# mLSTM and mixture of experts on one core: order of the gate activations, place of one gate broadcast, PSUM banks of the state update, and order of the w2 rounding

## The chip, the cores and the metric

One NeuronCore of one Trainium2 chip runs the program. The metric is the time of one execution on the device in microseconds (us). TensorE is called PE in the profile, VectorE DVE, ScalarE ACT, GpSimd POOL, and SyncE, which issues the DMA transfers, SP.

## The reference, cut to what matters

Sixteen heads (2 batches of 8) run a gated recurrence over 768 steps with 40 columns each; its output, normalised and gated by a sigmoid, is the input x (1536 rows of 320) of four dense experts, whose outputs are weighted and added.

```python
for t in range(S):                                   # S = 768, D = 40, 16 heads
    m_new = np.maximum(f_gate[:, :, t] + m, i_gate[:, :, t])
    f_stab = np.exp(f_gate[:, :, t] + m - m_new)
    i_stab = np.exp(i_gate[:, :, t] - m_new)
    m = m_new
    C = f_stab * C + i_stab * einsum('bhd,bhe->bhde', vt, kt)
    n = f_stab * n + i_stab * kt
    y[:, :, t] = sigmoid(o_gate) * (C @ q) / max(|n.q|, 1)
for e in range(E):                                   # 4 experts, F = 1024
    out += p[:, e:e+1] * (np.maximum(x @ w1[e], 0) @ w2[e])
```

## The kernel before

**Chunks.** The recurrence is cut into 12 chunks of 128 steps, numbered n = 0 to 11, with batch b = n % 2 and place in time c = n // 2. For a chunk, `spread(n)` (PE, for n = 0 to 3) or `load_f(n)` (a DMA that broadcasts from the DRAM copy `f_d`, for n >= 4) puts the forget gates of eight heads on all partitions (tile fb). `decay(n)` on DVE runs two scans over fb (four heads each, line 441) that give the decay matrix dd. `scores(n)` on PE multiplies k by q, `weigh(n)` on DVE multiplies by dd (tile pm), `intra(n)` on PE multiplies pm by the scaled values. `values(n)` and `keys(n)` on POOL scale v (tile vp) and k (tile kp). `state(n)` on PE adds the chunk to the state: its PSUM tile st is added on DVE (line 500, two instructions) to `cd`, the decayed old state from `carry` on POOL, and the sum is cs. `inter(n+1)` on PE reads the state of the other batch, and ACT scales it (yb, eight instructions). `norm(n)` on DVE makes the gated row block, `turn(n)` transposes it on PE (tile px), ACT rounds it to fp32r (xst, xd), and `turn_lo(n)` on DVE stores the remainder.

**Experts between the chunks.** While the recurrence runs, the first expert is computed for the finished rows: `PLAN[n]` lists what step n of the loop issues after its own chunk work. "H03" is `hidden` (products with w1, then `relu`) of row block 0, feature pair 3; "O00" is the output product with w2 for pair 0; "D" is one half of `decay(n + 2)`; "T" is `turn(n)`. All weights are held as a rounded value and a remainder: `split_w2` lets ACT write the rounded part (line 104) and POOL the remainder (line 107). After the loop the other row blocks and experts 1 to 3 follow.

**Order.** Each engine runs its instructions in the order in which the code issues them; nothing is reordered. Semaphores make one engine wait for another. PSUM tiles come in pairs from pools: tag "y" (`ps_y`) holds st, y1 of `inter` and y0 of `intra`, tag "w" (`ps_w`) holds the two tiles of `scores` and px of the loop's `turn`. A tile gets the slot whose last user came earliest, and waits for that user's readers.

**Activations.** ACT needs a table load (line 413 or 625 of the timeline) between Exp and Sigmoid; Copy and Relu run with either. Gates of the first chunks use Exp (lines 312, 322), then `gate_o(0)` a sigmoid of chunks 0 and 1, then Exp for the other chunks (line 625 and 322), and later sigmoids (`gate_o(1)` and on). `gate_o` works in place in acc: acc holds output gates until the rows' results replace them, and its rows 8 to 11 are filled by `load_o(4)` and `load_o(5)` late in the loop.

Of the kernel before, what the change touches and what calls it, by code (L numbers as in the profile page):

```python
# [18 lines left out]
L = 128  # L19
NC = S // L  # L20
# [15 lines left out]
NPE = 4  # L36

PLAN = {
    2: "H03 O00 T",
    3: "D O01 D O02 T",  # L40
    4: "D H10 D H11 O03 T",
    5: "D H12 D H13 O10 T",
# [14 lines left out]
def tile_mlstm_moe(ctx, tc, gt, qk, vk, ot, dp, w1, w2, out):  # L57
# [185 lines left out]
    with ExitStack() as actx:  # L243
# [56 lines left out]
        def gate_max(c0, c1):  # L300
            g = slice(c0 * L, c1 * L)
            nc.vector.tensor_tensor_scan(
                out=mb[:, c0 * L + 1:c1 * L + 1], data0=gat[:, 0, g], data1=gat[:, 1, g],
                initial=-1e30 if c0 == 0 else mb[:, c0 * L:c0 * L + 1],
                op0=ALU.add, op1=ALU.max,
            )
# [111 lines left out]
        def spread(n, pool, tag):  # L418

            b, c = n % B, n // B  # L420
            fbs[n] = [pool.tile([L, 4, L], F32, tag=tag, name="fb") for _ in range(2)]
            for h in range(H):
                nc.tensor.matmul(  # L423
                    fbs[n][h // 4][:, h % 4, :],
                    sel[:, b * H + h:b * H + h + 1].to_broadcast([L, L]),
                    fr[:, c * L:(c + 1) * L], start=True, stop=True,
                )

        def load_f(n):
            b, c = n % B, n // B  # L430
            fb = a0.tile([L, H, L], F32, tag=f"fb{n % 2}", name="fb")
            fbs[n] = fb[:, 0:4], fb[:, 4:8]
            nc.sync.dma_start(
                fb, f_d[b * H:(b + 1) * H, c * L:(c + 1) * L].unsqueeze(0).to_broadcast([L, H, L])
            )
# [41 lines left out]
            for r in range(2):  # L477
                nc.vector.tensor_mul(pm[:, r], ss[n][r], dd[:, r])  # L478

        def state(n, pool=ps_y, tag="y"):  # L480

            b, c, vv, kk = n % B, n // B, vvs[n], kp[n % 2]
            if c == NC - 1:
                return
            st = pool.tile([L, NP, L], F32, tag=tag, name="st")
            blocks = [(slice(64 * r, 64 * r + D), slice(64 * r, 64 * r + D + 1)) for r in range(2)]
            for p in range(NP):
                for r, (q, q2) in enumerate(blocks):
                    h = 2 * p + r
                    nc.tensor.matmul(  # L490
                        st[q, p, q2], kk[:, h], vv[:, h, 0:D + 1], start=True, stop=True
                    )
            cout = cs[b]
            if c == 0:
                for q, q2 in blocks:
                    copy(nc.scalar, cout[q, :, q2], st[q, :, q2])
            else:
                cd = cds.pop(n)
                for q, q2 in blocks:
                    nc.vector.tensor_add(cout[q, :, q2], cd[q, :, q2], st[q, :, q2])  # L500
# [107 lines left out]
        gate_pair(0, 1, nc.vector)  # L608
        nc.scalar.activation(even, par.unsqueeze(2).to_broadcast([L, 2, 64]), AF.Copy)
        gate_max(1, NC)  # L610
        spread(0, ps_h, "ph")
        spread(1, ps_o, "po")
        keep_warm(256, ps_w, "w")
        scores(0)
        gate_t(0, 1)
        pits.pop(0)
        g1, m1, mp1 = slice(L, S), mb[:, L + 1:S + 1], mb[:, L:S]
        nc.gpsimd.tensor_add(fs[:, g1], gat[:, 0, g1], mp1)
        values(0)
        values(1, HI)  # L620
        gate_o(0)
        decay(0)
        decay(1)
        nc.gpsimd.tensor_sub(fs[:, g1], fs[:, g1], m1)
        nc.scalar.activation(fs[:, g1], fs[:, g1], AF.Exp)
        for _ in range(2):
            keep_warm(256, ps_y, "y")
        scores(1, ps_h, "ph")
        weigh(0)
        weigh(1)  # L630
        gate_i(1, NC, nc.gpsimd)
        values(1, LO)
        intra(0)
        gate_starts(1, NC, nc.gpsimd)
        gate_pair(1, 2, nc.gpsimd)
        nc.sync.dma_start(f_d, fs)
        w2r = raws.tile([L, NF, DM], F32, tag="raw", name="w2r")
        nc.sync.dma_start(w2r, w2[0])
        load_vk(1)
        load_o(1)  # L640
        quarter_hi(0)
        quarter_lo(0)
        quarter_hi(1)
# [39 lines left out]
        keys(2)  # L683
        carry(2)
        first.corners(4)
        first.relu(4)
        inter(2, ps_o, "po")
        gate_o(1)
        split_w2(w2s, 0, 2, w2r, nc.gpsimd)
        gctx.close()  # L690
        a0 = actx.enter_context(
            tc.tile_pool(name="a0", bufs=1, side="right", reuse_waits="tile")
        )
        load_f(NPE)
        load_f(NPE + 1)

        def step(a):
            w, k = work[int(a[1])], int(a[2])
# [6 lines left out]
        for n in range(2, NCH):  # L705
            j, cc = n // 2, n % 2
            plan = PLAN[n].split()
            nxt = n + 1 < NCH
            if cc == 0 and j + 1 < NG:
                load_qk(j + 1)  # L710
                load_vk(j + 1)
            if NPE + 2 < n + 3 < NCH:
                load_f(n + 3)
            if cc == 0:
                if j > 1:
                    gate_o(j)
                if j + 1 < NG:
                    load_o(j + 1)
            if n == NCH - 2:
                raw1 = load_w1e(1)  # L720
            state(n)
            if n > 2:
                turn_lo(n - 1)
            if nxt:
                inter(n + 1)
            intra(n)
            norm(n)
            if n == 3:
                decay(NPE)
                load_f(NPE + 2)  # L730
            if nxt:
                scores(n + 1)
            for a in plan:
                if a[0] == "H":
                    work[int(a[1])].corners(int(a[2]) // 2 * 4)
                    break
            if nxt:
                values(n + 1)
                keys(n + 1)
                weigh(n + 1)  # L740
                carry(n + 1)
            if n < 4:
                for f in ((2, 4), (6,))[n - 2]:
                    split_w2(w2s, f, 2, w2r, nc.gpsimd)
            if n == 2:
                psum_e = const.tile([L, NCH, 1], F32, name="psum_e")
                nc.gpsimd.tensor_add(psum_e, pw[:, :, 0:1], pw[:, :, 1:2])
                for e in range(2, NE):
                    nc.gpsimd.tensor_add(psum_e, psum_e, pw[:, :, e:e + 1])
                nc.gpsimd.tensor_scalar_add(psum_e, psum_e, 1e-9)  # L750
            if n == 3:
                nc.vector.reciprocal(psum_e, psum_e)
                nc.gpsimd.tensor_mul(pw, pw, psum_e.to_broadcast([L, NCH, NE]))
            half = 0
            for a in plan:
                if a == "T":
                    turn(n, ps_w, "w")
                elif a == "D":
                    decay(n + 2, half)
                    half = 1  # L760
                else:
                    step(a)
# [103 lines left out]
```

## Time and profile before

| what | value |
|---|---|
| median of three runs | 413.05 us (412.98, 413.05, 414.2) |
| the profiled execution: its own time | 414.11 us |
| its span, first to last instruction | 412.3 us |
| PE busy | 400.2 us (97%) |
| DVE, ACT, POOL busy | 175.5, 130.0, 80.3 us |
| slices of the span (40 of 10.3 us) with a granted clock under nine tenths | one, the sixth (51.5 to 61.8 us): six tenths |

The span is shorter than the execution by 1.81 us. A busy share is a mean over stages: up to about 127 us the recurrence and the first expert share the engines, behind it only the experts are left.

### The profile page before, as it was taken

The page shows a single profiled execution, that of the slowest core. Times are in us where ns is not written, and L with a number is a line of the kernel's source. Part 1 is how long each engine was busy: PE and PEld are TensorE (multiplying, and loading weights), DVE is VectorE, ACT ScalarE, POOL GpSimd, SP SyncE. Part 2 cuts the span into 40 slices and gives each one's busy share as a digit, 9 for nine tenths or more (in the row PEclk, how much of TensorE's full clock was granted, in tenths as well). Part 3 has the DMA queues.
Part 4 walks back from the last instruction along what each step waited for, and adds up shares of the span by engine and source line. Part 5 has one row for each costly group of instructions (what it writes and reads, how often), then busy time and mean ns, then how long its engine had stood idle before and what let it go on. Part 6 is the DMA issues. An engine that isn't in the chain of part 4 may idle for free.

```text
span 412.3 us, 7152 instructions
## 1 busy us (share of the span) xinstructions
PE 400.2 (97%) x3042; PEld 361.9 (88%) x3042; DVE 175.5 (43%) x313; ACT 130.0 (32%) x312; POOL 80.3 (19%) x93
## 2 busy tenths in 40 slices
PE   9898599999999999999999999999999999999996
PEld 6698599989998898998988988989989889889896
DVE  7885977778842403313214134133142251231321
ACT  3958314444433533205213033034031140120210
POOL 2976722130000720002410010006100010000000
PEclk9999969999999999999999999999999999999999
DMA  6967457285000112100300003002100000001001
GB/s 175 338 225 202 123 159 198 85 232 203 3 2 2 58 70 102 52 2 0 129 0 2 0 2 153 2 0 74 55 0 2 0 2 32 33 0 50 16 16 49
DMA packets 15000, 29.34 MB, mean 71 GB/s; under 512 B 1000, under 2 KB 10760, under 8 KB 13656
## 3 DMA queue, kind: packets, MB, share of 16 engines
q1 hardware_dynamic: 14968, 28.88, 21.9%
q8 instruction: 24, 0.39, 0.4%
q14 instruction: 8, 0.07, 0.1%
HBM read 26.86 MB, written 2.02 MB: 70 GB/s over the span
## 4 chain that ended last, share of the span: by engine, by line
PE 87%; DVE 5%; issue 3%; POOL 2%; ACT 2%; DVEq 0%; POOLq 0%; ACTq 0%
PE ph L164 39%; PE po L224 39%; PE y L534 3%; PE s L472 2%; DVE dd L441 2%; PE pwm L84 1%; DVE cs L500 1%; PE fb L423 1%; POOL w1s L107 1%; PE px L561 1%; DVE pm L478 1%; POOL kp L461 1%; POOL cd L506 0%; PE st L490 0%; POOL w2s L107 0%
## 5 line engine op out<-in xcount | busy, mean ns | idle before, releaser
L164 PE MATMUL ph<-xst,w1s 128*128 128x512 f32 (+3 forms) x840 | 175.4, 365 | 0.2 <-DVE xst L569 0.2
L224 PE MATMUL po<-w2s,h 128*128 128x320 f32 x1152 | 173.3, 310 | 0.7 <-POOL w2s L107 0.7
L224 PEld LDWEIGHTS po<-w2s,h 128*128 128x128 f32 x1152 | 169.8, 188 | 2.4 <-POOL w2s L107 0.9
L164 PEld LDWEIGHTS ph<-xst,w1s 128*128 128x128 f32 (+1 forms) x840 | 142.1, 190 | 28.3 <-issue 4.4
L207 ACT ACTIVATE h<-ph 128x512 fp32r<-128x512 f32 x96 | 57.4, 599 | 206.1 <-PE ph L164 206.1
L208 DVE SCALAR_TENSOR_TENSOR h<-ph,h 128x512 fp32r<-128x512 f32 x96 | 66.1, 690 | 105.7 <-ACT h L207 105.2
L234 DVE SCALAR_TENSOR_TENSOR acc<-po,pw,acc 128x320 f32<-128x320 f32 x36 | 19.8, 551 | 99.9 <-PE po L224 99.9
L107 POOL TENSOR_TENSOR w1s<-raw,w1s 128x512 fp32r<-128x512 f32 (+1 forms) x24 | 23.6, 1023 | 96.9 <-ACT w1s L104 96.9
L441 DVE TENSOR_TENSOR_SCAN dd<-fb,id 128x512 f32<-128x512 f32 x24 | 30.4, 1293 | 0.1
L107 POOL TENSOR_TENSOR w2s<-raw,w2s 128x640 fp32r<-128x640 f32 x6 | 9.5, 1577 | 98.2 <-ACT w2s L104 98.2
L534 PE MATMUL y<-vp,pm 128*64 128x41 f32 x384 | 14.5, 237 | 6.5 <-DVE cs L500 5.5
L534 PEld LDWEIGHTS y<-vp,pm 128*64 128x64 f32 x384 | 13.3, 145 | 8.4 <-issue 4.0
L526 ACT ACTIVATE yb<-y,ibT 128x41 f32<-128x41 f32 x80 | 15.9, 311 | 1.5 <-ACT xd L565 1.0
L164 PE MATMUL ph<-xd,w1s 64*128 64x512 f32 (+1 forms) x56 | 16.2, 397 | 0.0
L478 DVE TENSOR_TENSOR pm<-s,dd 128x512 f32<-128x512 f32 x24 | 15.3, 682 | 0.1
L472 PE MATMUL s<-qk 64*128 64x128 f32 (+1 forms) x192 | 15.0, 296 | 0.0
L104 ACT ACTIVATE w2s<-raw 128x640 fp32r<-128x640 f32 x12 | 8.8, 733 | 16.5 <-DMA raw<-in_w 16.5
L455 POOL TENSOR_TENSOR vp<-vk,ibT 128x320 f32<-128x320 f32 x12 | 9.6, 799 | 22.3 <-PE y L534 12.8
L472 PEld LDWEIGHTS s<-qk 64*128 64x128 f32 (+1 forms) x192 | 12.8, 199 | 1.1 <-issue 0.7
L461 POOL TENSOR_TENSOR kp<-vk,dd 128x320 f32<-128x320 f32 x10 | 7.4, 740 | 23.8 <-DVE dd L441 23.8
L232 ACT ACTIVATE acc<-po,pw 128x320 f32<-128x320 f32 x12 | 6.3, 528 | 15.5 <-PE po L224 15.5
L104 ACT ACTIVATE w1s<-raw 128x512 fp32r<-128x512 f32 (+1 forms) x24 | 11.2, 517 | 0.0
(87 smaller groups left out, 187.1 us busy)
## 6 DMA issues: line engine op xcount, KB each, us to landing
raw<-in_w SPq DMA_DIRECT2D x3, 1536.0 KB, 8.8
fb<-f_d SPq DMA_DIRECT2D x8, 512.0 KB, 4.7
raw<-in_w SPq DMA_DIRECT2D x3, 1280.0 KB, 5.5
qk<-in_qk SPq DMA_DIRECT2D x4, 832.0 KB
vk<-in_vk SPq DMA_DIRECT2D x5, 640.0 KB, 10.1
acc<-in_ot SPq DMA_DIRECT2D x6, 320.0 KB, 9.9
out<-acc SPq DMA_DIRECT2D x12, 160.0 KB, 1.8
qk<-in_qk SPq DMA_DIRECT2D x4, 416.0 KB
```

Source lines behind the costliest of these rows:

```text
L104: nc.scalar.activation(hi, raw, AF.Copy)
L107: eng.tensor_sub(lo, raw, hi.bitcast(F32))
L164: nc.tensor.matmul(self.banks[i][:, f % self.nf, :], self.w1s[r, wi, f * L:(f + 1) * L], x[r, self.t0:self.t0 + self.n], start=(i not in s ...
L207: nc.scalar.activation(hh, ph, AF.Relu)
L208: nc.vector.scalar_tensor_tensor(out=hl, in0=ph, scalar=0.0, in1=hh.bitcast(F32), op0=ALU.max, op1=ALU.subtract)
L224: nc.tensor.matmul(po, self.hs[f][a][:, sl], ws[:, b, f, :], start=(first and i == 0), stop=(last and i == len(ks) - 1),)
L234: nc.vector.scalar_tensor_tensor(out=acc[:, i, :], in0=po, scalar=pw[:, i, e:e + 1], in1=acc[:, i, :], op0=ALU.mult, op1=ALU.add,)
L441: nc.vector.tensor_tensor_scan(out=dds[n][:, 4 * i:4 * i + 4].rearrange("p h t -> p (h t)"), data0=fbs[n][i].rearrange("p h t -> p (h t)") ...
L472: nc.tensor.matmul(ss[n][r][:, p, :], kg[q, p], qg[q, p], start=True, stop=True)
L478: nc.vector.tensor_mul(pm[:, r], ss[n][r], dd[:, r])
L526: nc.scalar.activation(yb[:, h], y1[:, h, 0:D + 1], AF.Copy, scale=ibT[:, c, i:i + 1])
L534: nc.tensor.matmul(y[t, h, 0:D + 1], pms[n][:, h, t], vvs[n][:, h, 0:D + 1], start=True, stop=True,)
```

## The change

It has five parts. (1) The exponentials of all chunks are issued before the first sigmoid, on POOL and ACT; `gate_t(0, 1)` moves between the two spreads; the v scaling of chunk 0 on POOL comes behind the gates' subtractions, and that of chunk 1 behind the gate pair; one more dummy product (`keep_warm`) stands before `scores(1)`. (2) The forget gates of chunk 4 are loaded early, into acc rows 8 to 11, so that `decay(4)` can run in step 2 of the plan; `decay(5)` alone stays in step 3. (3) `state(n)` takes a slot of tag "w", not "y". (4) `first.relu(4)` moves from ahead of the loop to behind `state(2)`. (5) The w2 roundings move: pair 0 ahead of the loop, pair 2 ahead of chunk 3's values in step 2, pair 4 ahead of chunk 4's in step 3, pair 6 behind them; the sum over the experts' probabilities moves one step back.

```diff
-    2: "H03 O00 T",
+    2: "D H03 D O00 T",
...
+        load_f(NPE, acc[:, 8:12].rearrange("p c d -> p (c d)")[:, 0:H * L]
+               .rearrange("p (h t) -> p h t", h=H))
...
-        def state(n, pool=ps_y, tag="y"):
+        def state(n, pool=ps_w, tag="w"):
...
         spread(0, ps_h, "ph")
+        gate_t(0, 1)
+        pits.pop(0)
         spread(1, ps_o, "po")
+        values(0, HI)
+        values(1, HI)
+        gate_f(1, NC, nc.gpsimd)
+        gate_i(1, NC, nc.gpsimd)
+        values(0, LO)
+        decay(0)
+        decay(1)
         keep_warm(256, ps_w, "w")
         scores(0)
...
-        for _ in range(2):
+        for _ in range(3):
             keep_warm(256, ps_y, "y")
         scores(1, ps_h, "ph")
+        gate_o(0)
...
-        first.relu(4)
         inter(2, ps_o, "po")
         gate_o(1)
...
             state(n)
-            if n > 2:
+            if n == 2:
+                first.relu(4)
+            else:
                 turn_lo(n - 1)
...
-            if n == 3:
-                decay(NPE)
-                load_f(NPE + 2)
...
+            if n == 2:
+                split_w2(w2s, 2, 2, w2r, nc.gpsimd)
+            if n == 3:
+                split_w2(w2s, 4, 2, w2r, nc.gpsimd)
             if nxt:
                 values(n + 1)
                 keys(n + 1)
```

On DVE, in step 2 and the start of step 3, the program before stands like this (from the weighting of chunk 3 to its norm; h is the remainder of a relu, line 569 and 570 are `turn_lo(2)`):

```order
L478 TENSOR_TENSOR pm<-s,dd 128x4x128 x2
L208 SCALAR_TENSOR_TENSOR h<-ph,h 128x512
L500 TENSOR_TENSOR cs_133<-cd,st 40x4x41 x2
L569 TENSOR_TENSOR xst<-px,xst 128x2x128
L570 TENSOR_TENSOR xst<-px,xst 64x128
L547 TENSOR_TENSOR y_678<-y_678,yb 128x8x41
```

and in the changed kernel:

```order
L479 TENSOR_TENSOR pm<-s,dd 128x4x128 x2
L442 SCALAR_TENSOR_TENSOR dd<-acc,id_121 128x512
L208 SCALAR_TENSOR_TENSOR h<-ph,h 128x512
L442 SCALAR_TENSOR_TENSOR dd<-acc,id_121 128x512
L501 TENSOR_TENSOR cs_133<-cd,st 40x4x41 x2
L570 TENSOR_TENSOR xst<-px,xst 128x2x128
L571 TENSOR_TENSOR xst<-px,xst 64x128
L548 TENSOR_TENSOR y_677<-y_677,yb 128x8x41
```

The two scans of `decay(4)`, which read the gates from acc, moved ahead of the state update of chunk 3 and of `turn_lo(2)`. They were behind the norm of chunk 3, ahead of the weighting of chunk 4.

On POOL, from the work of chunk 2 to the sum over the experts, the program before has these rows (vp, kp and cd of chunks 2, 3 and 4; w2s is a remainder of w2):

```order
L455 TENSOR_TENSOR vp_128<-vk,ibT 128x8x40
L461 TENSOR_TENSOR kp_130<-vk,dd 128x320
L506 TENSOR_TENSOR cd<-cs_132,bl 104x512
L107 TENSOR_TENSOR w2s_97<-w2r,w2s_97 128x640
L455 TENSOR_TENSOR vp_129<-vk,ibT 128x8x40
L461 TENSOR_TENSOR kp_131<-vk,dd 128x320
L506 TENSOR_TENSOR cd<-cs_133,bl 104x512
L107 TENSOR_TENSOR w2s_97<-w2r,w2s_97 128x640 x2
L747 TENSOR_TENSOR psum_e<-pw 128x12
```

and the changed kernel these:

```order
L456 TENSOR_TENSOR vp_128<-vk,ibT 128x8x40
L462 TENSOR_TENSOR kp_130<-vk,dd 128x320
L507 TENSOR_TENSOR cd<-cs_132,bl 104x512
L107 TENSOR_TENSOR w2s_97<-w2r,w2s_97 128x640 x2
L456 TENSOR_TENSOR vp_129<-vk,ibT 128x8x40
L462 TENSOR_TENSOR kp_131<-vk,dd 128x320
L507 TENSOR_TENSOR cd<-cs_133,bl 104x512
L107 TENSOR_TENSOR w2s_97<-w2r,w2s_97 128x640
L456 TENSOR_TENSOR vp_128<-vk,ibT 128x8x40
L462 TENSOR_TENSOR kp_130<-vk,dd 128x320
L507 TENSOR_TENSOR cd<-cs_132,bl 104x512
L107 TENSOR_TENSOR w2s_97<-w2r,w2s_97 128x640
```

Two w2 remainders now stand ahead of chunk 3's vp and kp, where there was one, and one each ahead of chunk 4's and behind it.

On ACT, the same stretch read before (yb of chunks 2 and 3, the sigmoid into acc, the w2 roundings):

```order
L207 ACTIVATE h<-ph 128x512
L526 ACTIVATE yb<-y_495,ibT 128x41 x8
L413 ACT_TABLE_LOAD
L413 ACTIVATE acc<-acc 128x640
L104 ACTIVATE w2s_97<-w2r 128x640
L526 ACTIVATE yb<-y_539,ibT 128x41 x8
L453 ACTIVATE vp_129<-ibT 128x8
L104 ACTIVATE w2s_97<-w2r 128x640 x2
```

and now, behind a first rounding of w2 that stands ahead of these rows:

```order
L527 ACTIVATE yb<-y_496,ibT 128x41 x8
L413 ACTIVATE acc<-acc 128x640
L207 ACTIVATE h<-ph 128x512
L527 ACTIVATE yb<-y_542,ibT 128x41 x8
L104 ACTIVATE w2s_97<-w2r 128x640
L454 ACTIVATE vp_129<-ibT 128x8
```

The table load is gone here, the relu came behind the first yb, and the rounding that the second POOL remainder needs stands behind the second yb.

## Rows read from the trace of the kernel before

**Rows 1.** Chain that ended last, its last stage: start, us, what.

```profile
127.77 14.05 PE ph L164 x62
...
409.17 0.55 DVE acc L234
```

**Rows 2.** Who waited for whom, PE: us in total, times, longest.

```profile
PE y L534 <- DVE cs L500: 5.5, 8, 3.7
...
PE px L561 <- DVE pm L478: 0.6, 1, 0.6
```

**Rows 3.** Timeline of PE: start, us, line, operation, idle before and its releaser.

```profile
40.68 1.16 PE L472 MATMUL s<-qk 64*128 64x128 f32 x16
...
51.56 1.93 PE L534 MATMUL y<-vp,pm 128*64 128x41 f32 x32 [3.67 <-DVE cs L500]
...
62.43 0.51 PE L490 MATMUL st<-vp,kp 128*40 128x41 f32 x16
...
63.87 1.13 PE L534 MATMUL y<-vp,pm 128*64 128x41 f32 x32 [0.19 <-DVE cs L500]
...
71.89 0.51 PE L490 MATMUL st<-vp,kp 128*40 128x41 f32 x16
```

**Rows 4.** One window: stretch, length, busy time of each engine, granted clock (PEclk), DMA.

```profile
52.00:53.00 1.00, 1.00 (x25) 1.00 (x23) 0.17 (x1) 0.00 (x0) 1.00 (x2) 0.50 0.99 203
```

**Rows 5.** Timeline of DVE, the decays of chunk 5 and what follows.

```profile
46.77 2.95 DVE L441 TENSOR_TENSOR_SCAN dd<-fb,id 128x512 f32<-128x512 f32 x1
...
49.64 1.22 DVE L441 TENSOR_TENSOR_SCAN dd<-fb,id 128x512 f32<-128x512 f32 x1
...
51.89 0.28 DVE L570 TENSOR_TENSOR xst<-px,xst 64x128 fp32r<-64x128 f32 x1
```

**Rows 6.** Timeline of POOL, the same stretch.

```profile
46.10 1.04 POOL L506 TENSOR_TENSOR cd<-cs,bl 104x512 f32<-104x512 f32 x1
47.09 1.54 POOL L107 TENSOR_TENSOR w2s<-w2r,w2s 128x640 fp32r<-128x640 f32 x1
...
49.74 1.63 POOL L455 TENSOR_TENSOR vp<-vk,ibT 128x320 f32<-128x320 f32 x1
```

**Rows 7.** Timelines of PE and DVE, the gates' stage.

```profile
9.96 1.16 PE L84 MATMUL pwm<-const-float32-0.0 128*128 128x256 f32 x4
...
15.63 0.17 DVE L548 TENSOR_SCALAR nq<-y 128x8 f32<-128x8 f32 x1 [0.64 <-PE y L534]
```

**Rows 8.** Timeline of ACT in step 2.

```profile
29.11 0.60 ACT L207 ACTIVATE h<-ph 128x512 fp32r<-128x512 f32 x1 [0.18 <-PE ph L164]
...
31.55 1.28 ACT L413 ACT_TABLE_LOAD   x1
...
33.49 0.72 ACT L104 ACTIVATE w2s<-w2r 128x640 fp32r<-128x640 f32 x1
34.12 1.58 ACT L526 ACTIVATE yb<-y,ibT 128x41 f32<-128x41 f32 x8
```

**Rows 9.** Timeline of POOL in step 2.

```profile
34.29 1.56 POOL L107 TENSOR_TENSOR w2s<-w2r,w2s 128x640 fp32r<-128x640 f32 x1 [4.34 <-ACT w2s L104]
...
36.48 0.75 POOL L461 TENSOR_TENSOR kp<-vk,dd 128x320 f32<-128x320 f32 x1
```

**Rows 10.** Timeline of PE, end of step 2.

```profile
35.90 2.03 PE L224 MATMUL po<-w2s,h 128*128 128x320 f32 x12 [0.67 <-POOL w2s L107]
...
38.18 0.51 PE L490 MATMUL st<-vp,kp 128*40 128x41 f32 x16
```

**Rows 11.** Timeline of DVE in step 2.

```profile
32.79 0.51 DVE L547 TENSOR_TENSOR y<-y,yb 128x328 f32<-128x328 f32 x1 [1.79 <-PE y L534]
...
35.00 1.28 DVE L478 TENSOR_TENSOR pm<-s,dd 128x512 f32<-128x512 f32 x2
37.56 0.69 DVE L208 SCALAR_TENSOR_TENSOR h<-ph,h 128x512 fp32r<-128x512 f32 x1 [1.28 <-ACT h L207]
```

**Rows 12.** DMA issues, the gate broadcasts: KB each, us to landing.

```profile
fb<-f_d SPq DMA_DIRECT2D x8, 512.0 KB, 4.7
```

More of the change, by code (lines that the diff above doesn't have):

```diff
@@ L427, in spread, with load_f @@
                 )
-        def load_f(n):
+        def load_f(n, fb=None):
             b, c = n % B, n // B
-            fb = a0.tile([L, H, L], F32, tag=f"fb{n % 2}", name="fb")
+            if fb is None:
+                fb = a0.tile([L, H, L], F32, tag=f"fb{n % 2}", name="fb")
             fbs[n] = fb[:, 0:4], fb[:, 4:8]
@@ L610, in tile_mlstm_moe @@
         gate_max(1, NC)
+        g1, m1, mp1 = slice(L, S), mb[:, L + 1:S + 1], mb[:, L:S]
         spread(0, ps_h, "ph")
+        gate_t(0, 1)
+        pits.pop(0)
         spread(1, ps_o, "po")
+        values(0, HI)
[5 more added lines that the diff above has]
+        decay(1)
         keep_warm(256, ps_w, "w")
         scores(0)
[L615 to L625, printed above, removed]
-        for _ in range(2):
+        for _ in range(3):
             keep_warm(256, ps_y, "y")
         scores(1, ps_h, "ph")
+        gate_o(0)
         weigh(0)
         weigh(1)
-        gate_i(1, NC, nc.gpsimd)
+        gate_starts(1, NC, nc.gpsimd)
+        gate_pair(1, 2, nc.gpsimd)
         values(1, LO)
         intra(0)
-        gate_starts(1, NC, nc.gpsimd)
-        gate_pair(1, 2, nc.gpsimd)
         nc.sync.dma_start(f_d, fs)
@@ L673, in tile_mlstm_moe @@
         scores(2)
-        state(0)
-        state(1)
+        state(0, ps_y, "y")
+        state(1, ps_y, "y")
         weigh(2)
+        split_w2_hi(w2s, 0, 2, w2r)
         spread(3, ps_o, "po")
@@ L685, in tile_mlstm_moe @@
         first.corners(4)
-        first.relu(4)
         inter(2, ps_o, "po")
         gate_o(1)
-        split_w2(w2s, 0, 2, w2r, nc.gpsimd)
         gctx.close()
@@ L693, in tile_mlstm_moe @@
         )
-        load_f(NPE)
         load_f(NPE + 1)
+        load_f(NPE + 2)
+        split_w2_lo(w2s, 0, 2, w2r, nc.gpsimd)
         def step(a):
@@ L711, in tile_mlstm_moe @@
                 load_vk(j + 1)
-            if NPE + 2 < n + 3 < NCH:
+            if n > 3 and n + 3 < NCH:
                 load_f(n + 3)
@@ L741, in tile_mlstm_moe @@
                 carry(n + 1)
[L742 to L745, printed above, removed]
+            if n == 3:
+                split_w2(w2s, 6, 2, w2r, nc.gpsimd)
                 psum_e = const.tile([L, NCH, 1], F32, name="psum_e")
@@ L750, in tile_mlstm_moe @@
                 nc.gpsimd.tensor_scalar_add(psum_e, psum_e, 1e-9)
-            if n == 3:
+            if n == 4:
                 nc.vector.reciprocal(psum_e, psum_e)
```

## The prediction

> **What bounds the kernel now.** I read the chain that ended last first. From 127.77 us it is PE alone, products behind products, down to the last addition on DVE at 409.17 us [rows 1]: nothing in the change touches that stage, so whatever it saves must reach PE before 127 us. There the list of waits says what to look for: `intra` waited for the state's addition (cs) on DVE eight times, 5.5 us in all, of which one wait is 3.7 us; the other seven share 1.8 us, about 0.2 each in most steps [rows 2]. The reader is to see why: st took a slot of the same pair as y0, so y0 had to wait until DVE had read st. The timeline shows the long one: `intra(4)` started only at 51.56 [rows 3]. Behind it comes a second loss. From 51.56 to `state(5)` at 62.43 PE took 10.87 us; from `intra(5)` at 63.87 to `state(6)` at 71.89 the same list of work took 8.02 [rows 3]. [...] So the stall in step 4 cost 3.67 and then 2.85 us more.
>
> Why was cs late? DVE had all four scans of `decay(4)` and `decay(5)` in step 3. One of them took 2.95 us, the next 1.22 [rows 5]. The long one began at 46.77 and ended at 49.72; POOL was in cd from 46.10, then in a w2 remainder until 48.63 [rows 6]. 48.63 and a scan of 1.2 make 49.8. So the scan waited for two POOL instructions that followed each other, and did its work then; the vp instruction at 49.74 in turn took 1.63 and ended when the second scan and some 0.7 of its own were over [rows 5, 6]. A scan whose gates lie in SBUF (both inputs there) thus excludes POOL, one at a time. [...]
>
> **Step by step.** Times are those of the profiled execution.
>
> *Gates.* DVE idled 0.64 us ahead of the norm of chunk 1, whose `intra` waited for POOL's v scaling [rows 7]; that comes earlier now. Against it stands one more dummy product, two instructions of 0.29 (1.16 for four) [rows 7], which delays `scores(1)` and the weighting. All exponentials ahead of the sigmoid save one table load of 1.28 on ACT [rows 8], but DVE's own chain (weighting, two norms) sets the end here, so it gives little. I take -0.2 us, between -0.64 and +0.4. [...]
>
> *Step 2, ACT and POOL.* yb of chunk 2 ended at 31.55, now 31.35. Then come the sigmoid (33.49 - 31.55 - 1.28 = 0.66), the moved relu (0.60) and yb of chunk 3, from 32.6, 1.58 long; then the rounding, 0.72 [rows 8]: POOL gets it at 34.75. POOL now has this remainder ahead of chunk 3's vp and kp: before, the same three ran from 34.29 to 37.23, 2.94 us [rows 9]. So kp is ready at 37.7. PE would be ready earlier: it loses the wait of 0.67 for the first w2 remainder [rows 10], which is made ahead of the loop now, the 0.2 of `intra(2)` and the 0.2 of the gates: 38.18 - 1.07 = 37.1. `state(3)` starts at 37.7, half a microsecond before its old place.
>
> *Step 2, DVE.* The moved relu's remainder now stands ahead of the norm of chunk 2 and waits for ACT's relu (31.35 + 0.66 + 0.60 = 32.6, and 0.69 on DVE): the norm starts at 33.3, not 32.79 [rows 8, 11]. The weighting follows 2.21 later (35.00 - 32.79) and takes 1.28: 36.8. There `decay(4)`'s first scan meets a POOL that is busy from 34.75 to 38.7 without a break (remainder, vp, kp, cd of 1.04 [rows 6]). As in rows 5 and 6 I let it wait for the instruction under way and one more, to the end of kp at 37.7; it ends at 38.9. The relu's remainder (0.69) follows to 39.6; cd, kept out until 38.9, holds POOL to 39.9; the second scan ends at 41.1; cs and `turn_lo(2)` take 1.31 (49.64 + 1.22 to 52.17 [rows 5]): 42.4. With st, scores and px in three turns on one pair of slots, `scores(4)` must wait for just these two. `intra(3)` is over at about 39.9, so PE idles for 2.5 us and `scores(4)` starts at 42.4, not 40.68 [rows 3]: 1.7 us lost.
>
> *Step 3.* Only `decay(5)` is left, behind the weighting. Before, from `scores(4)` (40.68) to the end of `inter(5)` (51.56 - 3.67 = 47.89) PE took 7.21, of which 0.6 was px waiting for the weighting [rows 2, 3]; that wait goes, since the weighting now comes ahead of both scans. `intra(4)` starts at 42.4 + 6.6 = 49.0, 2.56 earlier. DVE: norm 2.21 and weighting 1.28 bring 45.9; the scans meet the last w2 remainder (I add 0.9 of its 1.54) and take 2.4: 49.2; cs and `turn_lo(3)`: 50.5. `scores(5)` could start at 50.1, so it waits 0.4. From there the clock should hold, and to `state(5)` it is 8.02: 49.0 + 0.4 + 8.02 = 57.4, 5.0 before 62.43.
>
> *Steps 5 to 9.* The small waits go, 1.8 us less the two of steps 2 and 3 (0.2 each) and about 0.2 that `scores` waits for `turn_lo` instead: 1.2.
>
> *Edits at nothing.* The load of chunk 4's gates, 512 KB, lands 4.7 us after issue [rows 12]; it stands in SP's queue behind the DRAM copy of the gates and ahead of all loads of the loop, and its first reader comes at 36.8, in step 2. The whole stage from the first spreads to step 2 covers it; with no cover the scan would be 4.7 late. SP's later loads stand behind fewer waits than before, since the load for chunk 6 no longer waits for `decay(4)`. The rows of acc are written by `load_o(4)` only in step 6. The sum over probabilities fills a POOL that waits.
>
> Sum: 5.0 + 1.2 = 6.2. The span goes from 412.3 to 406.1; with 1.81 around it, 407.9 us. The profiled execution (414.11) lies 1.06 above the median 413.05; how long the low clock lasts may differ between runs, and I expect the changed kernel without that stretch, so I keep 407.9.
>
> **Rivals.**
> - *No collision.* If the first scan slips in between two POOL instructions, and the others too, 36.8 + 1.2 + 0.69 + 1.2 + 1.31 gives `scores(4)` at 41.2, `intra(4)` at 47.8 and no wait of `scores(5)`: `state(5)` at 55.8, gain 6.6 + 1.2 = 7.8, 406.3 us. Against it: POOL has no break there. Chance 0.18.
> - *The clock falls in step 3.* The idle time ahead of `scores(4)`, 2.5 us, lies between the 0.67 of rows 10, behind which no clock was lost, and the 3.67 of rows 3, which cost 2.85. If it falls, 407.9 + 2.85 = 410.8. Chance 0.19.
> - *Slower.* Place: the same stall. Once the clock is low, each microsecond of full-rate work costs one more. The gain of 6.2 is eaten when 6.2 us of work, 12.4 us on the wall, run at half rate, that is if it does not return by 54.8. The stretch of rows 3 and 4 lost 2.85, so it lasted about 5.7 on the wall. Two such stretches, the second set off by the wait of `scores(5)`, with a scan that waits for one POOL instruction more (1.0 late each time), make 407.9 + 5.7 + 2.0 = 415.6. Chance 0.09.
> - *The stall only moves.* DVE's total work is the same; if the lag of step 2 grows so that `scores(5)` waits as `intra(4)` did (3.67, and 2.85 of clock, less the 0.4 already counted), the time is 414.0: no change. Chance 0.06.
> - The forecast itself: 0.48.
>
> **The numbers.** A measurement of this kernel tells a difference from none above about 0.3%, 1.2 us. Faster: forecast, no collision and the lost clock, 0.85; same 0.06; slower 0.09. Range: the low end takes the no-collision case with the best gates term (406.3 - 0.4) and, should the 1.06 between profile and median hold here too, 404.9; the high end reaches the lost clock: 411.0. Outside remain the two last rivals and a little more.
>
> **What would show it.** Right: one table load on ACT ahead of 20 us besides the first, none at 31; the first w2 product without a wait; `scores(4)`, not `intra`, waiting for DVE; a scan of chunk 4 well over 1.2 us beside POOL's kp or cd; a clock at its upper level through 50 to 62 us; `state(5)` near 57. Wrong: `scores(4)` on time, or PE idle there for over 3 us and the 0.50 window back; `state(3)` later than 38.2, which would mean that the remainder ahead of kp costs more than computed.

## The result, and the profile after

The changed kernel takes 408.5 us (median of six runs, 407.57 to 409.75) against 413.25 of the kernel before: ratio 0.9883, 95% interval 0.986 to 0.9905. A second set of six runs, beside the experiments below, gave 409.6 (407.35 to 410.81), ratio 0.9905, 0.9877 to 0.9933. The profiled execution took 407.65, span 405.9; the forecast was 407.9 and 406.1. This execution is one of the faster ones, and the profiled one before, 414.11, one of the slower: their spans differ by 6.4 us, the medians of the two sets by 4.7 and 4.4.

The timeline of PE after the change (columns as in [rows 3]):

```profile
38.26 0.51 PE L491 MATMUL st<-vp,kp 128*40 128x41 f32 x16 [1.86 <-POOL kp L462]
...
41.24 2.57 PE L473 MATMUL s<-qk 64*128 64x128 f32 x16
...
49.91 1.08 PE L535 MATMUL y<-vp,pm 128*64 128x41 f32 x32
50.92 1.16 PE L473 MATMUL s<-qk 64*128 64x128 f32 x16
...
57.88 0.51 PE L491 MATMUL st<-vp,kp 128*40 128x41 f32 x16
58.22 0.91 PE L520 MATMUL y<-cs,qk 104*64 104x105 f32 x16
58.96 1.08 PE L535 MATMUL y<-vp,pm 128*64 128x41 f32 x32
...
66.95 0.51 PE L491 MATMUL st<-vp,kp 128*40 128x41 f32 x16
```

The wait of 3.67 us of [rows 3] is gone: `intra(4)` starts at 49.91 with no wait, and `state(5)` at 57.88, 4.55 earlier than 62.43. From there to `state(6)` it is 9.07 us; before it was 71.89 - 62.43 = 9.46. The one long wait left is 1.86 us, `state(3)` for POOL's keys of chunk 3. The timelines of DVE and of POOL show why:

```profile
34.78 1.28 DVE L479 TENSOR_TENSOR pm<-s,dd 128x512 f32<-128x512 f32 x2
35.98 1.70 DVE L442 TENSOR_TENSOR_SCAN dd<-acc,id 128x512 f32<-128x512 f32 x1
...
38.18 1.21 DVE L442 TENSOR_TENSOR_SCAN dd<-acc,id 128x512 f32<-128x512 f32 x1
40.26 0.66 DVE L501 TENSOR_TENSOR cs<-cd,st 40x164 f32<-40x164 f32 x2 [0.87 <-POOL cd L507]
...
44.78 4.70 DVE L442 TENSOR_TENSOR_SCAN dd<-fb,id 128x512 f32<-128x512 f32 x2
49.45 0.66 DVE L501 TENSOR_TENSOR cs<-cd,st 40x164 f32<-40x164 f32 x2
```

```profile
34.34 1.58 POOL L107 TENSOR_TENSOR w2s<-w2r,w2s 128x640 fp32r<-128x640 f32 x1 [3.39 <-DVE y L554]
35.88 0.72 POOL L456 TENSOR_TENSOR vp<-vk,ibT 128x320 f32<-128x320 f32 x1
36.56 1.65 POOL L462 TENSOR_TENSOR kp<-vk,dd 128x320 f32<-128x320 f32 x1
38.17 2.05 POOL L507 TENSOR_TENSOR cd<-cs,bl 104x512 f32<-104x512 f32 x1
...
44.91 1.97 POOL L507 TENSOR_TENSOR cd<-cs,bl 104x512 f32<-104x512 f32 x1
46.84 1.57 POOL L107 TENSOR_TENSOR w2s<-w2r,w2s 128x640 fp32r<-128x640 f32 x1
48.37 1.12 POOL L750 TENSOR_TENSOR psum_e<-pw 128x12 f32<-128x12 f32 x1
```

The first scan of `decay(4)` came to its turn at 35.98, while POOL was in vp, and took 0.5 us more than the second. It got in as vp ended; kp stood behind it and took 1.65 us where 0.75 is usual [rows 9]. The second scan started at 38.18, beside cd, and cd took 2.05 instead of 1.04 [rows 6]; the state's addition waited 0.87 for it. In step 3 the two scans of `decay(5)` took 4.70 us where two took 2.45 in a10 below, with POOL idle from 43.5 to 45.8. There cd waited for the first scan (1.97). The second scan alone:

```profile
45.96 3.53 DVE L442 TENSOR_TENSOR_SCAN dd<-fb,id 128x512 f32<-128x512 f32 x1
```

It waited for cd and then for the w2 remainder, until 48.41, and the first addition of the sum over the probabilities waited for it (1.12; 0.21 in the profile before). The exclusion is the one of [rows 5, 6]. Where a scan reads its gates from PSUM, none shows: in the profile before, the two scans of `decay(2)` took 2.30 us from 20.96 on, beside a w1 remainder on POOL that took 1.29 (1.28 at 16.17, with no scan beside it). Who goes first does not follow from the order of coming to the turn alone: the first scan of `decay(4)` came ahead of kp and kept it out, 0.9 us more in kp; the second scan of `decay(5)` came at 45.96, and the remainder, at 46.84, went ahead of it.

The windows of the same stretch (columns as in [rows 4]):

```profile
38.00:39.00 1.00, 0.74 (x26) 0.74 (x28) 1.00 (x2) 0.00 (x0) 1.00 (x2) 1.00 0.85 341
39.00:40.00 1.00, 1.00 (x24) 1.00 (x22) 0.39 (x1) 0.27 (x2) 1.00 (x1) 0.62 1.11 266
40.00:46.00 6.00, 6.00 (x50) 5.70 (x47) 5.54 (x14) 2.68 (x11) 4.19 (x5) 0.50 0.77 204
46.00:47.00 1.00, 1.00 (x8) 1.00 (x8) 1.00 (x2) 0.00 (x0) 1.00 (x2) 0.97 0.00 0
47.00:58.00 11.00, 11.00 (x147) 10.41 (x147) 10.58 (x18) 5.20 (x17) 7.89 (x11) 1.00 0.27 79
```

The granted clock fell to 0.50 behind the wait of 1.86 and was back soon after 46 (0.97 from 46 to 47); in [rows 4] it was at 0.50 in the window at 52 us, behind the wait of 3.67. At 0.50 `scores(4)` took 2.57 us, where 1.16 is its time at 1.00 [rows 3]. DVE is busy 5.54 us of the 6 in that stretch, and 10.58 of the 11 behind it. PE is busy all the time in both, so these windows alone do not say which of the two sets the pace; a5 below does.

### The profile page after: what moved, and what is told of

Its sections match the earlier page's. It is cut to its first block, busy times and chain, and to the rows that moved or that the text cites. A ratio compares the mean times of both kernels' runs of the same rounds, so it can differ in the third digit from the quotient of the medians.

```text
span 405.9 us, 7149 instructions
## 1 busy us (share of the span) xinstructions
PE 398.6 (98%) x3044; PEld 362.1 (89%) x3044; DVE 175.7 (43%) x313; ACT 127.7 (31%) x310; POOL 83.1 (20%) x93
## 4 chain that ended last, share of the span: by engine, by line
PE 93%; POOL 2%; DVE 2%; ACT 2%; DMA 1%; issue 0%; POOLq 0%
PE po L224 42%; PE ph L164 42%; PE s L473 3%; PE y L535 2%; PE y L520 2%; PE px L562 1%; PE st L491 1%; DMA gat<-in_gt 1%; DVE mb L302 0%; PE fb L423 0%; POOL kp L462 0%; ACT yb L527 0%; POOL w2s L107 0%; POOL fs L310 0%; ACT acc L413 0%
## 5 line engine op out<-in xcount | busy, mean ns | idle before, releaser
L207 ACT ACTIVATE h<-ph 128x512 fp32r<-128x512 f32 x96 | 57.4, 599 | 197.7 <-PE ph L164 197.7
L442 DVE TENSOR_TENSOR_SCAN dd<-fb,id 128x512 f32<-128x512 f32 x22 | 28.4, 1313 | 0.0
L473 PE MATMUL s<-qk 64*128 64x128 f32 (+1 forms) x192 | 16.0, 297 | 0.0
L462 POOL TENSOR_TENSOR kp<-vk,dd 128x320 f32<-128x320 f32 x10 | 8.3, 829 | 18.3 <-DVE dd L442 18.3
L456 POOL TENSOR_TENSOR vp<-vk,ibT 128x320 f32<-128x320 f32 x12 | 8.7, 723 | 15.6 <-PE y L535 8.5
```

The source lines that it names most:

```text
L207: nc.scalar.activation(hh, ph, AF.Relu)
L442: nc.vector.tensor_tensor_scan(out=dds[n][:, 4 * i:4 * i + 4].rearrange("p h t -> p (h t)"), data0=fbs[n][i].rearrange("p h t -> p (h t)") ...
L473: nc.tensor.matmul(ss[n][r][:, p, :], kg[q, p], qg[q, p], start=True, stop=True)
```

## The experiments

Each kernel was timed beside the kernel before on the same chip. "Range" is over the runs; the ratio is to the kernel before. Its median was 413.05 to 413.98 in these sets, so kernels of different sets are compared by their ratios; 0.001 is 0.4 us, and a difference of two ratios is uncertain by about 0.003.

| kernel | median us (range, runs) | ratio, 95% interval |
|---|---|---|
| a1_state_y | 410.1 (409.85 to 411.4, 6) | 0.9932, 0.9911 to 0.9953 |
| a2_decay_late | 411.6 (408.82 to 413.36, 12) | 0.9947, 0.9927 to 0.9966 |
| a3_pool_order | 407.4 (406.3 to 408.03, 5) | 0.9855, 0.9832 to 0.9878 |
| a4_gates_old | 409.7 (409.3 to 412.74, 12) | 0.9927, 0.9906 to 0.9947 |
| b1_state_w | 409.8 (409.35 to 411.06, 4) | 0.9907, 0.9886 to 0.9927 |
| a5_busy | 407.5 (407.29 to 409.2, 4) | 0.9856, 0.9834 to 0.9877 |
| a6_pool_free | 405.2 (404.06 to 406.15, 5) | 0.9795, 0.9773 to 0.9818 |
| a8_loads | 406.3 (404.07 to 407.13, 6) | 0.9807, 0.9779 to 0.9834 |
| a9_all | 406.3 (403.86 to 407.91, 6) | 0.9821, 0.9795 to 0.9847 |
| a10_busy2 | 404.2 (404.06 to 408.07, 6) | 0.9789, 0.9759 to 0.9819 |
| after_again | 409.6 (407.35 to 410.81, 6) | 0.9905, 0.9877 to 0.9933 |
| a11_busy_both | 407.3 (406.83 to 407.54, 5) | 0.986, 0.9842 to 0.9879 |

Three theories of what the change did were tested: **A**, DVE's chain of steps 2 and 3, lengthened where scans and POOL exclude each other, sets when PE goes on, and a lost clock lies hidden under it. **B**, what is left to lose is the lateness of chunk 3's keys and the clock. **C**, the gain came from the slot of the state. The move of the relu (part 4) and the old order of w2 (part 5) were not put back by themselves, and the early decay was not tried without the other parts.

### The slot undone, and the slot alone (a1_state_y, b1_state_w)

a1, in the changed kernel:

```diff
-        def state(n, pool=ps_w, tag="w"):
+        def state(n, pool=ps_y, tag="y"):
```

b1, in the kernel before:

```diff
-        def state(n, pool=ps_y, tag="y"):
+        def state(n, pool=ps_w, tag="w"):
-        state(0)
-        state(1)
+        state(0, ps_y, "y")
+        state(1, ps_y, "y")
```

> The changed kernel with one part undone: the state's PSUM tile takes a slot of tag y again. The changed kernel measured 408.5 us. Theory A (DVE's chain of step 3, lengthened by scans and POOL that exclude each other, sets when step 4 can go on): cs of chunk 4 is ready at about 50.1 us whatever the slot, so intra(4) waits for it as it did before, starts 0.2 later than its 49.9 and scores(5) no longer waits; the small waits of 0.2 to 0.36 a step of the later steps come back, 1.8 us in all. About 410 to 411 us. Theory C (the slot was the main cause of the gain; intra waited 3.67 us and lost 2.85 of clock because of it): most of 5 us comes back, 413 or more.

> The kernel before with one part of the change alone: from chunk 2 on the state's PSUM tile takes a slot of tag w. Theory A (DVE's chain of step 3 sets the end of the stall): intra(4) no longer waits, but the next product that needs a slot, scores(5), waits for the same DVE instructions, so the stall of 3.67 us shrinks only by intra's own 1.1 and the clock is lost all the same; the small waits of the later steps go, 1.3 to 1.85. About 410.5 to 412 us against 413.9 of the kernel before. Rival C (the slot is the main cause): the stall and the lost clock both go, 5 us or more: 409 or less.

Measured: a1 410.1, as A said; b1 409.8, better than A and short of C. A's place for a1's wait was wrong. In its profile (411.11 us) `intra(3)` waited 1.56 us for cs and the clock fell behind that (0.50 from 42 to 46 us); `intra(4)` waited only 0.18. The timeline of PE in a1, a later step:

```profile
59.78 0.91 PE L520 MATMUL y<-cs,qk 104*64 104x105 f32 x16
60.88 1.13 PE L535 MATMUL y<-vp,pm 128*64 128x41 f32 x32 [0.19 <-DVE cs L501]
```

`intra` starts 1.10 behind `inter`, after the change 0.74 (58.22 to 58.96). The idle time shown is 0.19, the delay 0.36. The timeline of PE in b1:

```profile
46.82 1.11 PE L534 MATMUL y<-vp,pm 128*64 128x41 f32 x32
50.49 0.46 PE L472 MATMUL s<-qk 64*128 64x128 f32 x2 [2.56 <-DVE cs L500]
...
59.63 0.51 PE L490 MATMUL st<-vp,kp 128*40 128x41 f32 x16
```

The stall moved to `scores(5)` and shrank to 2.56, as A said. The clock fell as well, but was at 0.50 from 52 to 55 us only, before the change from 52 to 58; A had not counted on that. The rest of b1's gain is 0.39 a step (to 9.07), and in this profile its work began earlier: `products` of block 0 at 18.26, not 19.22, with the same code ahead of it; the dummy products that open the program took 3.19 us from 1.75 on, in the profile before 4.05. So two profiles of the same code can differ by a microsecond in their first stage. The parts overlap: the slot alone is worth 0.9% to the kernel before, which is most of what the whole change gains (1.2 and 1.0% in its two sets), and yet taking it from the changed kernel costs only a quarter to half a per cent (0.9932 against 0.9905 and 0.9883). Among runs at a mean clock (the granted clock over the whole run) of 0.999 or 1.000 that cost is plainer: 409.9 to 410.3 in a1, 407.4 to 407.6 in the changed kernel. C is right that the slot alone gets most of the gain, and wrong that the gain hangs on it: the other parts shorten the same stall.

### Chunk 4's decay back in step 3 (a2_decay_late)

```diff
-    2: "D H03 D O00 T",
+    2: "H03 O00 T",
...
             norm(n)
+            if n == 3:
+                decay(NPE)
```

> The changed kernel with the two scans of chunk 4's decay behind the norm of chunk 3 again, in step 3; the early load of its gates stays. Theory A: DVE has the same work up to the state update of chunk 4, and in step 2 the scans cost as much by exclusion (POOL's keys and carry became 0.9 and 1.0 us longer) as they save in step 3; the time is that of the changed kernel within a microsecond, 407.5 to 409.7, with state(3) near 37.3 and scores(4) near 39.5, and a wait of scores(5) or its weighting of 1 to 2 us in its place. Rival (the early decay is what removed the stall of 3.67): the stall returns ahead of scores(5), 3 us or more, and with it the lost clock: 411 to 414.

Measured 411.6: the rival, not A, though the stall ahead of `scores(5)` is 2.59 us, less than the rival's 3. PE and DVE in its profile:

```profile
52.33 2.31 PE L473 MATMUL s<-qk 64*128 64x128 f32 x14 [2.59 <-DVE cs L501]
```

```profile
38.18 0.66 DVE L501 TENSOR_TENSOR cs<-cd,st 40x164 f32<-40x164 f32 x2 [1.67 <-POOL cd L507]
...
42.35 3.69 DVE L442 TENSOR_TENSOR_SCAN dd<-acc,id 128x512 f32<-128x512 f32 x2
...
47.35 4.28 DVE L442 TENSOR_TENSOR_SCAN dd<-fb,id 128x512 f32<-128x512 f32 x2
```

My error was to hold DVE's work for constant and therefore its end: without the scans DVE idles 1.67 us ahead of cs in step 2, and the scans then take 7.97 us of step 3. The early decay uses idle time; that is worth about 2 us (0.9947 against 0.9883 and 0.9905: 2.6 and 1.7). Behind the wait of 2.59 the granted clock is 0.50 from 52 to 58 us, and there PE sets the pace: from `scores(5)` to `state(5)` it is 10.1 us (62.44 - 52.33), after the change 6.96.

### POOL's order, and POOL kept free (a3_pool_order, a6_pool_free)

```diff
-            if n == 2:
-                split_w2(w2s, 2, 2, w2r, nc.gpsimd)
-            if n == 3:
-                split_w2(w2s, 4, 2, w2r, nc.gpsimd)
             if nxt:
                 values(n + 1)
                 keys(n + 1)
                 weigh(n + 1)
                 carry(n + 1)
+            if n == 2:
+                split_w2(w2s, 2, 2, w2r, nc.gpsimd)
             if n == 3:
-                split_w2(w2s, 6, 2, w2r, nc.gpsimd)
+                split_w2(w2s, 4, 2, w2r, nc.gpsimd)
...
+            if n == 4:
+                split_w2(w2s, 6, 2, w2r, nc.gpsimd)
```

The removed line of pair 6 and the last two lines are a6 alone: a3 keeps pair 6 in step 3, behind pair 4; a6 moves it to step 4, and the sum over the probabilities to step 2.

> The changed kernel with the w2 remainders of pairs 2 and 4 on POOL behind the values, keys and carry of the next chunk, not ahead of them. Theory B (the lateness of chunk 3's keys, and the clock that PE loses by its wait of 1.86 us, cost what the prediction missed): state(3) starts near 36.4 us without a wait, the granted clock stays up through 39 to 46, and the time is 405 to 406.5. Theory A: state(3) also starts without a wait, but DVE's chain is shorter only by what the first scan waited, 0.5 us, and the second meets the moved remainder: 407.5 to 408.5. If the order on POOL is no matter: 408.5 within 0.3.

> The kernel with w2 remainders 2 and 4 behind the values and keys (407.4 us), and besides that the sum over the experts' probabilities in step 2 and w2 pair 6 in step 4, so that POOL has little to do beside the two scans of chunk 5's decay. These took 4.7 to 4.8 us where two scans alone take 2.4. Theory A: the scans fall to about 2.7 us, cs of chunk 4 comes 2 us earlier, intra(4) near 48.3; 405 to 405.9 us. Rival (exclusion on the chain is no matter, since chunk 4's q and k arrive late and hold PE by 2.5 us first): 407 to 407.7.

Measured: a3 407.4 (0.9855 against 0.9883 and 0.9905: 1.2 and 2.1 us less), at the lower edge of A's range and above B's. Its runs do not part the two theories: the two at a mean clock of 1.000 took 406.3 and 406.4, in B's range, the other three 407.4 to 408.0. `state(3)` starts at once, but another wait comes to light (PE of a3), and in a6 the scans of `decay(5)` shrink (DVE of a6):

```profile
36.28 0.51 PE L491 MATMUL st<-vp,kp 128*40 128x41 f32 x16
39.25 0.94 PE L520 MATMUL y<-cs,qk 104*64 104x105 f32 x16 [2.46 <-DMA qk<-in_qk]
```

```profile
43.31 3.33 DVE L442 TENSOR_TENSOR_SCAN dd<-fb,id 128x512 f32<-128x512 f32 x2
```

The q and k of chunk 4 are issued at 28.5 us in a3, in a6 and in the changed kernel. In a3's profile PE waited 2.46 for them, and the clock fell behind that (0.50 from 41 to 47 us); in a6's it waited 0.3, and in the changed kernel's, where `inter(4)` comes to its turn only at 38.60, not at all. So a3's gain is partly lost again. a6, 405.2, is what A said: 4.83 us of scans in a3 became 3.33, where A had 2.7. All its runs (404.06 to 406.15) lie below those of a3, but how much of the 2.2 us between the medians is the scans and how much that q and k came earlier in some runs, these two profiles do not say.

### The gates' old order (a4_gates_old)

The code from the first spread to the DRAM copy of the gates is that of the kernel before, in the core (moves of `values` and `keep_warm` left out):

```diff
-        gate_f(1, NC, nc.gpsimd)
-        gate_i(1, NC, nc.gpsimd)
...
         scores(0)
...
+        gate_o(0)
...
+        nc.gpsimd.tensor_sub(fs[:, g1], fs[:, g1], m1)
+        nc.scalar.activation(fs[:, g1], fs[:, g1], AF.Exp)
...
-        gate_o(0)
...
+        gate_i(1, NC, nc.gpsimd)
```

> The changed kernel with the order of the gates' exponentials and sigmoids of the kernel before. The prediction's term was -0.2 us for this part, the profile of the changed kernel shows products(0) 0.5 earlier. Theory A (ACT's second table load, 1.28 us, comes back ahead of the relu and norm of step 2, which now stand in DVE's chain): slower by 0.5 and up to 1.3 more, 409.3 to 410.3. Rival (table loads are off the path): slower by 0.5 or less, 408.5 to 409.0.

Measured 409.7, in A's range, with three of twelve runs above 412. The profile is of one of these (412.14). The timelines of ACT, DVE and PE in it:

```profile
31.89 1.28 ACT L413 ACT_TABLE_LOAD   x1
```

```profile
34.44 0.69 DVE L208 SCALAR_TENSOR_TENSOR h<-ph,h 128x512 fp32r<-128x512 f32 x1 [3.11 <-ACT h L207]
```

```profile
40.50 0.75 PE L491 MATMUL st<-vp,kp 128*40 128x41 f32 x16 [2.18 <-POOL kp L462]
```

The load stands ahead of the relu, DVE waits 3.11 for it (1.68 after the change), and `state(3)` is 2.24 late, of which 0.84 comes from the gates' stage (`intra(2)` at 31.10, not 30.26) and 1.4 from ACT. The 1.4 is the load's. The 0.84 is not shown to be the order's: PE was slow there in this profile (px at 17.14 took 0.87 us and two dummy products 1.06, in the profile before 0.52 and 0.60), and b1, with the old order too, has `intra(2)` at 29.80. With the new order ten profiles have it at 30.10 to 30.36. By the ratios (0.9927 against 0.9883 and 0.9905) the part is worth 0.9 or 1.8 us, hardly more than the noise; what the profile shows of it lies in step 2.

### Filling PE's idle time (a5_busy, after_again, a11_busy_both)

```diff
-            for k in range(3):
+            for k in list(range(3)) * (5 if n == 2 else 1):
                 r = slice(k * L, min((k + 1) * L, DM))
                 nc.tensor.transpose(px[0:r.stop - r.start, k, :], xrs[n][:, r], ident)
```

This is a5, on the changed kernel; a11 has `n in (2, 3)` for `n == 2`; after_again is the changed kernel unaltered. The twelve added transposes of a step write the same values again.

> The changed kernel with the three transposes of turn(2) issued five times over, so that PE is busy up to the time when chunk 3's keys are ready and does not idle for 1.86 us there. Theory A (the lost clock lies under DVE's chain): the granted clock stays at its upper level from 39 to 46 us, but scores(5) then waits for the state update at about 50.5 and the time is that of the changed kernel within a microsecond: 407.5 to 409.5. Theory B (the lost clock is what the prediction did not count, 2.85 us): 405.5 to 406.5.

> The changed kernel itself, unaltered, beside the two others on the same chip: 407.5 to 409.8 us, a ratio to the kernel before of 0.986 to 0.9905 as in the first comparison.

> The changed kernel with the transposes of turn(2) and of turn(3) issued five times over: filling for PE ahead of state(3), which waited 1.9 us for POOL, and ahead of scores(5), which waited 1.3 us for DVE. Twelve runs of the changed kernel lie between 407.35 and 410.81 us; those at a mean granted clock of 0.999 or 1.000 at 407.35 to 407.57, most of the others at 409 to 410.8. Theory A': the difference is the clock that falls at one of the two waits, above all the second, behind which DVE's chain hides nothing; with PE busy at both, all runs take 407.2 to 407.8. Rival (the spread has another source, or the clock falls in spite of the filling): runs above 409 remain, median 408.5 to 409.5.

a5 took 407.5, as A said. Its clock stays up in the profile (1.00 from 38 to 62 us), and yet `scores(5)` starts at 50.23 and `state(5)` at 57.84 (57.88 in the profile of the changed kernel): the fall behind `state(3)` had been hidden under DVE. The profile of the changed kernel's second set shows the same from the other side. PE, and one window over the whole stretch:

```profile
38.10 0.51 PE L491 MATMUL st<-vp,kp 128*40 128x41 f32 x16 [1.85 <-POOL kp L462]
...
49.97 0.46 PE L473 MATMUL s<-qk 64*128 64x128 f32 x2 [1.11 <-DVE cs L501]
...
57.59 0.51 PE L491 MATMUL st<-vp,kp 128*40 128x41 f32 x16
```

```profile
38.00:58.00 20.00, 17.73 (x252) 16.50 (x254) 18.13 (x33) 8.43 (x29) 15.53 (x18) 1.00 0.47 131
```

Here the clock did not fall behind a wait of 1.85 us, PE was early, and `scores(5)` waited 1.1 and 0.2 for DVE. The time was 407.35. Other runs of this set, with a mean clock of 0.991 or 0.992, took 410.1 to 410.8; in the first set three at that clock took 407.65, 408.05 and 409.0, and the first of these is the profile in which the fall is hidden. With both waits filled (a11) all five runs lie at 406.8 to 407.5, at a clock of 0.999 or 1.000. So the spread of the changed kernel comes from the clock and from the place where it falls. That it falls behind the wait of `scores(5)` in the runs above 410 is inferred, not shown: the clock did fall there in b1 and a4 (waits of 2.56 and 1.78; 0.50 from 52 to 54 in b1, 0.56 from 54 to 56 in a4), but no profile of the changed kernel caught it.

### Loads, and an earlier decay (a8_loads, a10_busy2, a9_all)

```diff
-        load_f(NPE + 1)
-        load_f(NPE + 2)
...
                 load_qk(j + 1)
                 load_vk(j + 1)
+            if n == 2:
+                load_f(NPE + 1)
+                load_f(NPE + 2)
```

This is a8, on top of a6. a10 is a8 with the transposes of `turn(2)` five times over, as in a5. a9 is a8 with

```diff
-    2: "D H03 D O00 T",
+    2: "H03 O00 T",
...
         split_w2_lo(w2s, 0, 2, w2r, nc.gpsimd)
+        decay(NPE, 0)
...
             if n == 2:
+                decay(NPE, 1)
                 first.relu(4)
```

> The same kernel as a6_pool_free with the gate broadcasts of chunks 5 and 6 issued behind the loads of chunks 4 and 5's q, k and v, not ahead of them. With remainders 2 and 4 moved, inter(4) waited 2.46 us for q and k, issued at 28.5 us and landing at 39.2. Theory A: they land near 36.5, inter(4) follows state(3) without a wait, and the norm of chunk 3 starts when cs and turn_lo(2) are done, about 1.3 us earlier; 403.7 to 405. Rival (the DMA queues are full whatever the order, and the late load moves to another tile): no gain over a6_pool_free within 0.4 us.

> a8_loads with the transposes of turn(2) issued five times over, as filling for PE ahead of scores(4). a8_loads took 404.1 us in two runs at a mean granted clock of 1.000 and 407.1 in three runs at 0.992; its profile, one of the latter, shows the clock fall behind 1.3 us of waits ahead of scores(4). Theory A': the lost clock is hidden only where DVE's chain is longer than PE's; in a8_loads that chain is short enough for the loss to count whole, 3 us. With PE busy there the clock holds: all runs at 403.8 to 404.8. Rival (the clock falls for another reason, or costs nothing): the same two groups, median 405.5 to 407.

> The kernel with POOL kept free and the loads reordered (a8_loads), and besides that the two scans of chunk 4's decay earlier still: the first ahead of the loop, the second ahead of the relu's remainder in step 2, where DVE idles 1.9 and 1.7 us. Theory A (DVE's chain of steps 2 and 3 sets the end; its idle time is what an early decay can use): scores(4) follows intra(3) without a wait near 38.4 us, intra(4) starts near 45, and PE has no idle time behind which the clock could fall: 402 to 403.5 us, in all runs. Rival (from here PE or another queue is the bound, or the scans now hold up chunk 2's state): 404 or more, as a8_loads in its better runs.

In a8 `inter(4)` follows `state(3)` at once. Two runs took 404.1, inside A's range, one 405.6, and three 407.1, which neither theory had. The profile, one of the latter, PE and a window:

```profile
39.44 0.46 PE L473 MATMUL s<-qk 64*128 64x128 f32 x2 [1.10 <-DVE cs L501]
40.10 1.99 PE L473 MATMUL s<-qk 40*128 40x128 f32 x14 [0.20 <-DVE xst L571]
```

```profile
40.00:46.00 6.00, 5.90 (x29) 5.67 (x30) 5.51 (x11) 0.00 (x0) 3.73 (x5) 0.52 0.50 132
```

The clock fell behind waits of 1.1 and 0.2, and now DVE, with its scans down to 2.50, waited for PE (3.30 ahead of the next cs): 3.0 us lost against the two runs at a clock of 1.000. a10 fills that wait. DVE, and the same window:

```profile
43.23 2.45 DVE L442 TENSOR_TENSOR_SCAN dd<-fb,id 128x512 f32<-128x512 f32 x2
```

```profile
40.00:46.00 6.00, 5.90 (x66) 5.50 (x67) 5.62 (x12) 1.72 (x8) 3.51 (x5) 1.00 0.66 158
```

Five of its six runs lie at 404.06 to 404.18; one took 408.07 at 0.995, unexplained. This version is ahead of both kernels, of the one before by 2.1% (1.8 to 2.4%). a9 (406.3) went the other way than A expected:

```profile
29.59 3.22 DVE L442 TENSOR_TENSOR_SCAN dd<-acc,id 128x512 f32<-128x512 f32 x1 [1.61 <-POOL cd L507]
32.73 0.65 DVE L501 TENSOR_TENSOR cs<-cd,st 40x164 f32<-40x164 f32 x2
```

The scan met POOL's w2 remainder and vp, took 3.22, and put off the state's addition of chunk 2; `scores(3)` waited 1.7 for that, and the clock fell there (0.51 from 34 to 36 us, 0.64 from 36 to 38). Here DVE's idle time was of no use to the scan, because POOL did not idle too.

## Why the prediction was right, and where its steps were not

The time, the sign and the main mechanism were right: the stall of `intra(4)` went, and the waits moved to `scores`, for DVE. The sum 6.2 was 6.4 between the two profiled executions (412.3 - 405.9), but so close a match is partly luck: over the medians the gain is 4.7 and 4.4, where the forecast (407.9 against 413.05) had 5.2. Step by step:

- *Gates*, -0.2: undoing the part cost 0.9 or 1.8 us (a4, by the ratios to either set). The failed step is "DVE's own chain sets the end here, so it gives little". For the gates' stage nothing contradicts it; in step 2 the change puts the relu behind the sigmoid, and there the load of 1.28 would have been ahead of DVE's chain. The prediction's times for ACT in step 2 had the load left out, without counting that as a gain of this part.
- *`state(3)` at 37.7*: 38.26 and 38.10. The failed step is "I let it wait for the instruction under way and one more": the scan waited for vp alone, and kp for the scan. The sign named for this (`state(3)` later than 38.2) is in the first profile, but not for the reason given there: the remainder ahead of kp took 1.58, no more than computed.
- *`scores(4)` at 42.4, with 2.5 us idle*: 41.24 with no wait, at a clock of 0.50; 40.91 with waits of 0.65 and 0.21, at 1.00. The scans were done 1.7 us earlier than computed, so the gap was a third. The sign that `scores(4)` would wait for DVE came in the second profile alone.
- *`intra(4)` at 49.0*: 49.91 and 47.78. *`scores(5)` waits 0.4*: 0 and 1.32. *`state(5)` at 57.4*: 57.88 and 57.59. Two errors cancelled: step 2 cost DVE less, step 3 more, since the scans of `decay(5)` met cd and the last remainder and took 4.70, not 3.3. There the step "the instruction under way and one more" held, for the second scan. The sum over the probabilities, put down as an edit at nothing, waited for that scan and not the other way round.
- *Steps 5 to 9*, +1.2: 6.4 - 4.55 = 1.85. The mechanism was right; the term was sized too small by reading the shown idle of 0.19 a step, where the wait delays the start by 0.36.
- *The clock holds*: in some runs (a mean of 0.999 or 1.000 in three of twelve). The rival of the lost clock gave 410.8; the runs above 410 are this rival, probably at another place, behind `scores(5)` (inferred, see above). Behind `state(3)` the loss is hidden (407.65 with the fall, 407.35 without), which the prediction did not think of.
- *No collision, slower, the stall only moves*: none of them came. The reserve that "no collision" spoke of is real: with POOL's work moved away it is 405.2 (a6), and 404.2 with the loads reordered and PE's gap filled as well (a10).
- *The load of chunk 4's gates, at nothing*: right in that its scan never waited. But loads behind it come late: chunk 4's q and k held PE for 2.46 us in a3 and 0.34 in a6.

## What to carry to other kernels

A slot or an order that takes one wait away shows the next chain behind it: ask which engine's chain ends there, and whether the moved work falls into that engine's idle time (a2 against the change: about 2 us) or beside an engine that holds it up (in a9 a scan took 3.22 us beside POOL's work; in a6, with less beside them, two took 3.33 where a3 had 4.83). Read the price of a small wait from the distance between starts with and without it, not from the idle time shown (0.36 against 0.19 in a1). Where TensorE idles ahead of dense work, for times as here (1.3 to 2.6 us), count the clock as a chance of losing up to the 3.0 us by which a8's runs differ; repeated products in the gap can be cheaper than the risk (median 404.2 in a10, 406.3 in a8).

## What was not expected of the hardware

- The same wait of PE was followed by a fall of the granted clock in one execution (1.86 us; 0.50 from 40 to 46) and by none in another (1.85 us; 1.00 from 38 to 58); in a8 the clock fell behind waits of 1.1 and 0.2 us (0.52 from 40 to 46), while the same two ahead of `scores(5)` in the second profile of the changed kernel had no fall behind them (1.00). A fall cost 3.0 us where PE set the pace (404.1 against 407.1 in a8), at most 0.3 where DVE did (407.65 against 407.35). What decides it is open.
- When scan and POOL instructions meet, the loser changes. Before, a scan lost 1.7 us to two POOL instructions; after, kp and cd lost 0.9 and 1.0 to two scans in step 2, and in step 3 a scan lost 2.3 to cd and a remainder again. What decides it is open.
- The q and k of chunk 4, issued at 28.47 us in a3 and at 28.53 in a6, let `inter(4)` start at 39.25 and at 37.18: 2.07 us apart. The DMA share was 0.97 from 34 to 38 us in a3 and 1.02 from 38 to 40 in a6.
